# A tuned attention-and-MLP kernel: two token tiles of batch 1 as a quad of seven half-size products

## The chip, the cores and the metric

The kernel runs on one core of a Trainium2 chip. The metric is the device time of one execution in microseconds (us); several runs are made and their median is compared. Differences under about half a microsecond are close to what such runs can tell.

## The reference, cut to what matters

Four batches, eight heads, 768 tokens, head size 64, so a model width of 512. A block-sparse attention feeds an MLP over tokens and then over channels:

```python
scores = scale * q @ k^T                      # (4, 8, 768, 768), masked by blocks of 32
attn   = softmax(where(mask, scores, -1e9));  x = attn @ v        # (4, 768, 512)
a1  = alpha1 * x + beta1
tok = einsum('ts,bsd->btd', w_tok, a1);       u = x + lam * tok
a2  = alpha2 * u + beta2
ch  = maximum(a2 @ w_ch1, 0) @ w_ch2          # 512 -> 2048 -> 512
out = u + lam * ch
```

The change is in the last product, `relu(...) @ w_ch2`, of batch 1. `lam` is folded into the weights of that product beforehand (line 783), so a tile's product is simply added to `x_sb`, which holds u.

## The kernel before, in words

**Pairs and score groups.** Two heads are worked on at a time: 16 pairs, four to a batch. From pair 5 on, a pair is three *score groups*, and each group has three units of scores. TensorE writes the first unit into two tiles of the pool `mm` (two matmuls of 512 columns, or four of 256), and the other two into tiles of the pool `sp`. ScalarE takes the exponential (line 619): two instructions of 128x512 for the `mm` pair, one of 128x1024 for each `sp` tile. VectorE multiplies each result `eT` by the mask (line 636), TensorE multiplies by v (line 671, 12 or 24 short matmuls into `op`), VectorE normalises into `x_sb` (lines 688, 689).

**Around them**, for the same or an earlier batch: the token product (line 846, 12 matmuls, called L846 here), its addition and cast (lines 858, 865), a transposing DMA `uraw<-ubf` on SyncE's queue (line 898), the scaling of what it brings (line 889, "uscale"), the first MLP product (line 919, four matmuls of 384 columns) with its ReLU on ScalarE (line 926), and the second MLP product (line 1058). The first MLP product of a batch has 32 pieces; a piece of it is called **f** here. The second, done directly, has for each of the six token tiles four pieces of four matmuls of 512 columns, called **g**; after the fourth VectorE adds the bank to `x_sb` (line 1067) and SyncE stores the tile (line 1071).

**Order.** There is no run-time choice: each engine takes its instructions in the order of emission. That order is written out by hand in `WEAVE`, one string of letters per score group. `W1` is for pairs 5 to 7, `W2` for pairs 8 to 11, `W2L` for pairs 12 to 15, `W3` for the rest. The letters that matter here: `q` scores of a group and the first exponential; `x` the next exponential; `k` a mask multiply; `p` a product with v; `f` and `g` the next piece of the first and second MLP product; `S` and `A` one VectorE sum for the quads (activations, weights); `Y` the copy of v; `T` a token product; `v` a uscale; `d` a transposing DMA; digits are planned odd jobs. Batch 1's MLP runs inside `W2` (its f pieces begin in the fifth string) and the beginning of `W2L`.

**Quads.** For batches 2 and 3 the kernel takes two token tiles together (before: tile t and t+3) and does the 2x2 block product in seven products in place of eight, each of eight matmuls of 256 columns (lines 1160 and 1170). It needs four sums of activations on VectorE (line 1144: two new tiles, X1 and X2, and two in place), four sums of the weights, T1 to T4 (line 1098, done once), and after each product an addition to `x_sb` (line 1180). Products 1, 6 and 5 build on one another in one bank, products 7 and 4 in another. Between two of them VectorE reads the bank, and the next must wait for that read.

**Banks.** The pool `mm` has three banks of PSUM, `sp` two tiles of two banks, `op` one. All of this shares `mm`: the first unit of every score group (two tiles), every f, every g, every token product. Which bank a tile gets is settled when the program is built; a tile waits until the last reader of its bank is done.

```python
    def mm_tile(shape=(P, DM), dt=FP):
        return psum.tile(list(shape), dt, name="mm", tag="mm", bufs=3)
```

Of the kernel before, what the change touches and what calls it, by code (L numbers as in the profile page):

```python
# [18 lines left out]
B = 4  # L19
H = 8  # L20
S = 768
# [4 lines left out]
DM = 512  # L26
P = 128
NT = S // P
# [38 lines left out]
]  # L67
W2L = [
# [18 lines left out]
]  # L87
STR = (2, 3)
HN = NH // 2
HC = DM // 2  # L90
FS = 6
# [157 lines left out]
def kernel(  # L249
# [16 lines left out]
    nc = tc.nc  # L266
# [194 lines left out]
    def sp_tile():  # L461
        return psum.tile([P, 2, 512], FP, name="sp", tag="sp", bufs=2)
# [6 lines left out]
    def mm_tile(shape=(P, DM), dt=FP):  # L469
        return psum.tile(list(shape), dt, name="mm", tag="mm", bufs=3)  # L470
# [103 lines left out]
    x_sbs = {}  # L574
# [540 lines left out]
    def a_of(b, t, name, r=slice(0, HN)):  # L1115
        if name in ("X1", "X2"):
            return xs[(b, t, name)][:, r]
        c, half = {"11": (0, 0), "12": (0, 1), "21": (1, 0), "22": (1, 1)}[name]
        return hts[(b, c)][:, HN * half + r.start : HN * half + r.stop, ts(t, P)]

    SOP = {
        1: ("X1", "21", "22", ALU.add),
# [5 lines left out]
    def job_s(b, t, n, r=slice(0, HN)):  # L1128
        dst, a, c, op = SOP[n]
        rows = range(r.start, r.stop)  # L1130
        for name in (a, c):
            if name[0] == "X":
                assert all(("S", b, t, int(name[1]), m) in did for m in rows)
            else:
                h, half = divmod(int(name) - 11, 10)
                assert all(("f", b, h, HN * half + m) in did for m in rows)
# [7 lines left out]
        nc.vector.tensor_tensor(  # L1144
            out=a_of(b, t, dst, r), in0=a_of(b, t, a, r), in1=a_of(b, t, c, r), op=op
        )
        did.update(("S", b, t, n, m) for m in rows)
# [8 lines left out]
        7: ("21", "T3", 3),  # L1156
    }
    banks = {}

    def mul(b, t, n, ps, start, cols=slice(0, HC)):  # L1160
        a, m, need = PROD[n]
        assert m in bq or all((m, r) in did for r in range(0, HN, 2))
        if need:
            assert all(("S", b, t, need, r) in did for r in range(HN))
        c, half = {"1": (0, 0), "X": (1, 0)}.get(a[0], (1, 0))
        if need == 0:
            h, half = divmod(int(a) - 11, 10)
            assert all(("f", b, h, HN * half + r) in did for r in range(HN))
        for r in range(HN):
            nc.tensor.matmul(  # L1170
                ps,
                a_of(b, t, a)[:, r],
                b_rows(m, r)[:, 0, cols],
                start=(start and r == 0),
                stop=(r == HN - 1),
                skip_group_check=True,
            )

    def plus(x, ps):
        nc.vector.tensor_tensor(out=x, in0=x, in1=ps, op=ALU.add)  # L1180

    def twice(ps):
        return ps.unsqueeze(1).broadcast_to([P, 2, HC])
# [1 line left out]
    lo, hi = slice(0, HC), slice(HC, DM)  # L1185

    def job_p(b, t, n):
        x = x_sbs[b]
        last = (b, t) == (B - 1, NT // 2 - 1)
        bk = banks.setdefault((b, t), {})  # L1190
        if n in (1, 2, 7):
            bk[n] = sp_tile()[:, 0] if n == 1 else mm_tile()[:]
        if n == 3 and not last and 2 not in bk:
            bk[2] = mm_tile()[:]
        if n == 1:
            mul(b, t, 1, bk[1][:, lo], True)
            plus(x[:, t, lo], bk[1][:, lo])
        elif n == 2:
            mul(b, t, 2, bk[2][:, lo], True)
            if last or b < B - 1:  # L1200
                plus(x[:, t, lo], bk.pop(2)[:, lo])
            if last:
                emit_store(b, t, lo)
        elif n == 6:
            mul(b, t, 6, bk[1][:, lo], False)
            plus(x[:, t + 3, lo], bk[1][:, lo])
        elif n == 7:
            mul(b, t, 7, bk[7][:, lo], True)
            plus(x[:, t + 3, hi], bk[7][:, lo])
        elif n == 5:  # L1210
            mul(b, t, 5, bk[1][:, lo], False)
            plus(x[:, t : t + 4 : 3, hi], twice(bk[1][:, lo]))
        elif n == 4:
            mul(b, t, 4, bk[7][:, lo], False)
            plus(x[:, t + 3, lo], bk[7][:, lo])
            emit_store(b, t + 3, slice(0, DM))
        elif last:
            for h in range(2):
                sl = slice(HC + h * P, HC + h * P + P)
                ps = (mm_tile(), op_tile([P, DM]))[h]  # L1220
                mul(b, t, 3, ps[:, sl], True, ts(h, P))
                plus(x[:, t, sl], ps[:, sl])
                emit_store(b, t, sl, (nc.sync, nc.scalar)[h])
        else:
            sl = hi if b < B - 1 else slice(0, DM)
            mul(b, t, 3, bk[2][:, hi], b < B - 1)
            plus(x[:, t, sl], bk[2][:, sl])
            emit_store(b, t, slice(0, DM))
        did.add((b, t, n))

    NPAIR = B * NP
# [34 lines left out]
    def start_mlp(b):  # L1266
# [16 lines left out]
        ]  # L1283
        todo["S"] += [lambda t=t, n=n, r=r: job_s(b, t, n, r) for t, n, r in S_ORDER[b]]

    REST = (6, 7, 5, 4, 3)
    P_ORDER = {
        2: [(0, g, "g") for g in range(4)]
        + [(t, 2) for t in (1, 2)]
        + [(3, g, "g") for g in range(4)]  # L1290
        + [(t, 1) for t in (1, 2)]
        + [(t, n) for t in (1, 2) for n in REST],
        3: [(t, n) for t in range(2) for n in (1, 2)]
        + [(t, n) for t in range(2) for n in REST]
        + [(2, n) for n in (1, 2) + REST],
    }
    ALL, R1, R2 = slice(0, HN), slice(0, HN // 2), slice(HN // 2, HN)
    S_ORDER = {
        2: [(t, n, ALL) for t in (1, 2) for n in (1, 2, 3, 4)],
        3: [(t, n, R1) for n in (1, 2, 3) for t in range(3)]  # L1300
        + [(t, n, r) for t in range(3) for n, r in ((1, R2), (2, R2), (3, R2), (4, ALL))],
    }

    def start_pair(i):
# [227 lines left out]
```

## Time and profile before

| | |
|---|---|
| median of 3 runs | 298.61 us (298.6 to 298.87) |
| the profiled execution | 298.76 us |
| its span in the profile | 297.1 us, so 1.66 us lie around the span |
| granted TensorE clock | 1.0 throughout |
| TensorE busy | 289.7 us, 98% of the span |
| VectorE, ScalarE, GpSimd busy | 237.8, 217.1, 109.8 us |

A row of a timeline gives the start, the busy time, the engine, the line and operation, the tiles, and how many instructions were merged; in brackets stands the idle time of the engine before it and what ended that. Ends of matmuls are modelled, so the busy time of a row reaches a little into the next row; the spacing of the starts is what a piece costs.

The score groups of the stretch in question are numbered here by their start on TensorE in the profile before: G1 at 134.56 us, G2 142.44, G3 148.73 (these are pair 10), G4 154.89, G5 159.38, G6 164.88 (pair 11, the end of `W2`), G7 170.21, G8 173.69, G9 184.40 (pair 12, the beginning of `W2L`), G10 188.21, G11 191.54, G12 196.74.

### The profile page before, as it was taken

To read this page: it belongs to the slowest core of one execution; us is meant where nothing else is said; L and a number is where in the kernel's file an instruction comes from. 1 tells how busy PE (TensorE), PEld (TensorE's weight loads), DVE (VectorE), ACT (ScalarE), POOL (GpSimd) and SP (SyncE) were. 2 spreads that over 40 slices of the span, in tenths; PEclk is the share of its full clock that TensorE was granted. 3 is DMA by queue.
4 is the path that set the end of the run, shared out by engine and by line. 5 is a ranking of instruction groups with operands and counts; after the bars stand their busy time and mean duration, and the time that the engine had idled before them with its cause. 6 is when DMAs were issued, how large, how long until landed. Compare 5 with 4: busy or idle time off the path is not lost.

```text
span 297.1 us, 7554 instructions
## 1 busy us (share of the span) xinstructions
PE 289.7 (98%) x3082; PEld 193.5 (65%) x3101; DVE 237.8 (80%) x485; ACT 217.1 (73%) x324; POOL 109.8 (37%) x149
## 2 busy tenths in 40 slices
PE   8999999999999999999999999999999999999995
PEld 3688888665567565565576466556576679665884
DVE  4988899995678796977878777895956899799774
ACT  4999999998899963999779581999869744576000
POOL 8997978632443710355323340335320300000000
PEclk9999999999999999999999999999999999999999
DMA  6999999992392995729955767745520211400032
GB/s 182 184 199 186 192 171 187 171 123 44 95 147 55 112 203 84 118 65 119 125 96 73 124 110 146 103 92 69 70 62 17 38 38 29 141 1 3 0 141 73
DMA packets 57274, 31.09 MB, mean 105 GB/s; under 512 B 37204, under 2 KB 54016, under 8 KB 57240
## 3 DMA queue, kind: packets, MB, share of 16 engines
q0 software_dynamic: 16752, 14.22, 34.4%
q1 hardware_dynamic: 40020, 15.92, 29.3%
q8 instruction: 24, 0.39, 0.6%
q10 hardware_dynamic: 468, 0.47, 0.5%
q14 instruction: 10, 0.08, 0.1%
HBM read 29.75 MB, written 6.29 MB: 121 GB/s over the span
## 4 chain that ended last, share of the span: by engine, by line
PE 84%; DVE 6%; DMA 4%; ACT 3%; issue 1%; POOL 1%; SPq 0%; POOLq 0%
PE mm L919 18%; PE mm L1058 13%; PE sp L601 10%; PE mm L846 8%; PE op L671 7%; PE mm L1170 5%; PE sp L1170 4%; PE mm L601 3%; DVE eT L636 3%; PE mm L822 3%; PE op L648 2%; DMA vr<-in_v_dram 2%; ACT eT L619 2%; PE mm L1016 2%; PE sp L1016 2%; DMA uraw<-ubf 2%
## 5 line engine op out<-in xcount | busy, mean ns | idle before, releaser
L619 ACT ACTIVATE eT<-sp,expb 128x1024 f16<-128x1024 f32 x111 | 118.4, 1120 | 2.1 <-PE sp L601 1.4
L636 DVE TENSOR_TENSOR eT<-eT,mask 128x1024 f16<-128x1024 f16 x99 | 80.6, 843 | 13.5 <-ACT eT L619 13.3
L919 PE MATMUL mm<-uT,w1b 128*128 128x384 bf16 x416 | 76.8, 326 | 0.4 <-ACT hts L926 0.3
L705 POOL TENSOR_TENSOR a1pp<-x_sb,vbc 128x384 bf16<-128x384 f32 x25 | 28.5, 1138 | 119.0 <-DVE x_sb L689 84.7
L619 ACT ACTIVATE eT<-mm,expb 128x512 f16<-128x512 f32 x66 | 41.7, 685 | 26.5 <-PE mm L601 26.3
L926 ACT ACTIVATE hts<-mm 128x384 bf16<-128x384 f32 x104 | 49.1, 502 | 13.3 <-PE mm L919 12.4
L919 PEld LDWEIGHTS <-w1b 128*128 128x128 bf16 x416 | 38.7, 98 | 26.4 <-issue 2.9
L1058 PE MATMUL mm<-w2b,hts 128*128 128x512 bf16 x205 | 52.2, 379 | 0.9 <-issue 0.2
L671 PEld LDWEIGHTS <-eT 128*128 128x128 f16 x792 | 29.8, 98 | 8.8 <-issue 1.7
L1058 PEld LDWEIGHTS <-hts 128*128 128x128 bf16 x224 | 19.8, 98 | 22.3 <-issue 3.9
L671 PE MATMUL op<-vext,eT 128*128 128x65 f16 x792 | 32.1, 194 | 0.4 <-DVE x_sb L689 0.3
L601 PE MATMUL sp<-qTs,kTs 88*128 88x512 bf16 (+1 forms) x120 | 26.9, 325 | 1.2 <-ACT eT L619 0.7
L706 POOL TENSOR_TENSOR a1pp<-a1pp,vbc 128x384 bf16<-128x384 bf16 x25 | 26.7, 1069 | 2.0
L846 PE MATMUL mm<-a1pp,wtokT 128*128 128x256 bf16 x216 | 25.9, 273 | 0.1
L846 PEld LDWEIGHTS <-wtokT 128*128 128x128 bf16 x216 | 20.6, 98 | 5.6 <-issue 1.8
L1170 PEld LDWEIGHTS <-hts 128*128 128x128 bf16 x208 | 19.5, 98 | 3.0 <-issue 0.3
L858 DVE TENSOR_TENSOR x_sb<-x_sb,mm 128x512 f32<-128x512 f32 x18 | 12.3, 686 | 9.9 <-PE mm L846 9.8
L601 PE MATMUL sp<-qhT,khT 64*128 64x256 bf16 (+1 forms) x176 | 19.8, 322 | 0.0
L601 PEld LDWEIGHTS <-khT 64*128 64x128 bf16 x264 | 10.6, 94 | 12.7 <-issue 9.2
L648 PEld LDWEIGHTS <-eT 128*128 128x128 f16 x360 | 14.9, 97 | 3.8 <-issue 0.3
L689 DVE TENSOR_TENSOR x_sb<-op,rcp 128x384 f32<-128x384 f32 x28 | 15.6, 558 | 1.0
L1067 DVE TENSOR_TENSOR x_sb<-x_sb,mm 128x512 f32<-128x512 f32 x14 | 9.6, 686 | 8.2 <-PE mm L1058 6.7
(135 smaller groups left out, 376.9 us busy)
## 6 DMA issues: line engine op xcount, KB each, us to landing
out_dram<-x_sb SPq DMA_DIRECT2D x23, 256.0 KB
qpad<-in_q_dram POOLq DMA_DIRECT2D x15, 192.0 KB, 4.6
kr<-in_k_dram POOLq DMA_DIRECT2D x15, 192.0 KB, 5.3
vr<-in_v_dram POOLq DMA_DIRECT2D x15, 192.0 KB, 6.3
w1b<-in_moe_w_ch_dram POOLq DMA_DIRECT2D x4, 512.0 KB, 9.2
w2b<-in_moe_w_ch_dram POOLq DMA_DIRECT2D x4, 512.0 KB, 7.7
hts<-in_moe_w_tok_dram POOLq DMA_DIRECT2D x2, 576.0 KB, 8.7
x_sb<-in_k_dram ACTq DMA_DIRECT2D x2, 192.0 KB
```

The lines of the kernel that those rows point to most:

```text
L601: nc.tensor.matmul(sp[jj][:, dst], lhsT, rhs, start=True, stop=True, skip_group_check=True,)
L619: nc.scalar.activation(dst, at, AF.Exp, bias=expb[:], scale=SCALE)
L636: nc.vector.tensor_mul(out=e, in0=e, in1=keep)
L648: nc.tensor.matmul(op[0][:, o, :], ets[u][:, jj, h * QB + n * P : h * QB + n * P + P], vexts[i % NVB][:, w, 2 * jp + jj, :], start=op[1] == 0,
L671: nc.tensor.matmul(op[0][:, o, :], ets[u][:, jj, h * QB + n * P : h * QB + n * P + P], vexts[i % NVB][:, w, 2 * jp + jj, :], start=op[1] == 0,
L705: eng.tensor_tensor(out=dst, in0=x_sbs[b][:, :, cols], in1=bc[0], op=ALU.mult)
L706: eng.tensor_tensor(out=dst, in0=dst, in1=bc[1], op=ALU.add)
L846: nc.tensor.matmul(ps[:, o], wtokT[:, os_, ts(2 * n + o, P)], a1pps[i][:, os_, :], start=(os_ == 0 and o == 0), stop=(os_ == NT - 1 and o ...
L919: nc.tensor.matmul(ps[:, 0:QC], w1b[:, dk, ts(n, P)], uTs[b][:, dk, ts(c, QC)], start=(dk == 0), stop=(dk == 3),)
L926: nc.scalar.activation(h_row(b, c, n), ps[:, 0:QC], AF.Relu)
L1058: nc.tensor.matmul(ps[:], ht[:, nk, ts(o % 3, P)], w2b[:, nk, :], start=(nk == 0), stop=(nk == NH - 1),)
L1170: nc.tensor.matmul(ps, a_of(b, t, a)[:, r], b_rows(m, r)[:, 0, cols], start=(start and r == 0), stop=(r == HN - 1), skip_group_check=True,)
```

## The change

Batch 1's tiles 0 and 1 become a quad; tiles 2 to 5 stay direct. The quads are now named by their two tiles, `(0, 1)`, `(1, 4)` and so on, where before `t` stood for `(t, t + 3)`; the quads of batches 2 and 3 do the same work as before. The new quad's products 1, 6 and 5 use a bank of the pool `mm`, where the older quads use one of `sp`. The strings of `W2` from the seventh on, and two of `W2L`, are rewritten:

- G1: two f come sooner in place of two g; one S.
- G2: two f in place of two g; one S at the end.
- G3: a g (now product 2) at its end.
- G4: the three A move away, two S and two g (products 1 and 6) come in.
- G5: three g (product 5 and two pieces of tile 2) and no f, before three g and two f.
- G6: three A come in; four g (the last two pieces of tile 2, products 7 and 3) and no f, before four g and one f.
- G7: two g (product 4, the first piece of tile 3) and no f, before one g and one f.
- G11: no g, before one.

```diff
 W2 = [
 ...
-    "q f L f 0 f k A A A A A A A A 1 f Y x f p g x f p f g k k 2",
-    "q x k x k Q 0 g 1 s f f g p 2 p f f k p",
-    "q T 0 k f 1 x k f T x f 2 p k K p",
-    "q A A A x 0 x T k 1 k f 2 k f Q f d p L",
-    "q x 0 x K k g d k s f g f 1 k p p g 2",
-    "q Y g x x k g k f 0 1 k 2 p g v g v",
+    "q f L f 0 f k A A A A A A A A 1 f f S Y x f p f x f p f k k 2",
+    "q x f k x f k Q 0 1 s f f p 2 p f f k S p",
+    "q T 0 k f 1 x k f T x f 2 p k K p g",
+    "q S S g x 0 x T k g 1 k f 2 k f Q f d p L",
+    "q x 0 x K k g d k s g 1 k p p g 2",
+    "q Y A A A g x x k g k 0 1 k 2 p g v g v",
 W2L = [
-    "q 0 p p g k x L x p f k 1 K 2 k",
+    "q 0 p p g k x L x p g k 1 K 2 k",
 ...
-    "q 0 p 1 g x k f K k x f p p k 2 f",
+    "q 0 p 1 x k f K k x f p p k 2 f",
 ...
-STR = (2, 3)
+STR = (1, 2, 3)
 ...
+    LATE = [(2, (1, 4)), (2, (2, 5))] + [(3, (o, o + 3)) for o in range(3)]
 ...
-        if n in (1, 2, 7):
-            bk[n] = sp_tile()[:, 0] if n == 1 else mm_tile()[:]
-        if n == 3 and not last and 2 not in bk:
-            bk[2] = mm_tile()[:]
+        if n == 1 and (b, t) in LATE:
+            bk[1] = sp_tile()[:, 0]
+        elif n in (1, 2, 7) or (n == 3 and not tail):
+            bk[n] = mm_tile()[:]
 ...
     P_ORDER = {
+        1: quad((0, 1), (2, 1, 6, 5))
+        + direct(2)
+        + quad((0, 1), (7, 3, 4))
+        + direct(3, 4, 5),
 ...
     S_ORDER = {
+        1: [((0, 1), n, ALL) for n in (1, 2, 3, 4)],
```

More of the change, by code (lines that the diff above doesn't have):

```diff
@@ L1117, in a_of, with a_ready @@
             return xs[(b, t, name)][:, r]
-        c, half = {"11": (0, 0), "12": (0, 1), "21": (1, 0), "22": (1, 1)}[name]
-        return hts[(b, c)][:, HN * half + r.start : HN * half + r.stop, ts(t, P)]
+        o, half = t[int(name[0]) - 1], int(name[1]) - 1
+        return hts[(b, o // 3)][:, HN * half + r.start : HN * half + r.stop, ts(o % 3, P)]
+    def a_ready(b, t, name, rows):
+        if name[0] == "X":
+            return all(("S", b, t, int(name[1]), m) in did for m in rows)
+        o, half = t[int(name[0]) - 1], int(name[1]) - 1
+        return all(("f", b, o // 3, HN * half + m) in did for m in rows)
     SOP = {
@@ L1130, in job_s @@
         rows = range(r.start, r.stop)
[L1131 to L1136, printed above, removed]
+        assert a_ready(b, t, a, rows) and a_ready(b, t, c, rows)
         if n == 3:
@@ L1164, in mul @@
             assert all(("S", b, t, need, r) in did for r in range(HN))
[L1165 to L1168, printed above, removed]
+        assert a_ready(b, t, a, range(HN))
         for r in range(HN):
@@ L1221, in job_p @@
                 mul(b, t, 3, ps[:, sl], True, ts(h, P))
[L1222 to L1228 removed]
+                plus(x[:, o1, sl], ps[:, sl])
+                emit_store(b, o1, sl, (nc.sync, nc.scalar)[h])
+        else:
+            assert {(b, t, m) for m in (1, 2, 5)} <= did
+            sl, ps = (slice(0, DM), bk[2]) if tail else (hi, bk[3])
+            mul(b, t, 3, ps[:, hi], not tail)
+            plus(x[:, o1, sl], ps[:, sl])
+            emit_store(b, o1, slice(0, DM))
         did.add((b, t, n))
```

56 lines of the change are left out of this document (34 added, 22 removed).

## The prediction

> **What bounds the kernel now.** The first part of the page, the busy times, comes first: TensorE has no room.
>
> ```profile
> span 297.1 us, 7554 instructions
> PE 289.7 (98%) x3082; PEld 193.5 (65%) x3101; DVE 237.8 (80%) x485; ACT 217.1 (73%) x324; POOL 109.8 (37%) x149
> ```
>
> A busy share can hide waits, so the chain of waits gives the price of each piece, and the timeline of TensorE the starts of the score groups.
>
> ```profile
> 112.88 1.31 PE mm L846 x12
> 125.15 1.30 PE mm L919 x8
> 154.23 0.73 PE op L671 x24
> 182.74 1.73 PE mm L1058 x8
> 248.18 0.87 PE sp L1170 x8
> ```
>
> ```profile
> 135.32 3.42 PE L919 MATMUL mm<-uT,w1b 128*128 128x384 bf16 x20
> 142.44 0.39 PE L601 MATMUL mm<-qhT,khT 64*128 64x512 bf16 x2
> 142.66 0.60 PE L601 MATMUL sp<-qhT,khT 64*128 64x256 bf16 x6
> 148.73 0.39 PE L601 MATMUL mm<-qhT,khT 64*128 64x256 bf16 x4
> 170.21 0.39 PE L601 MATMUL mm<-qhT,khT 64*128 64x512 bf16 x2
> 173.69 0.39 PE L601 MATMUL mm<-qhT,khT 64*128 64x512 bf16 x2
> 184.40 0.39 PE L601 MATMUL mm<-qhT,khT 64*128 64x256 bf16 x4
> 195.25 0.91 PE L671 MATMUL op<-vext,eT 128*128 128x65 f16 x24 [0.25 <-DVE x_sb L689]
> 196.74 0.39 PE L601 MATMUL mm<-qhT,khT 64*128 64x256 bf16 x4
> ```
>
> An f costs 0.65 us, a g 0.865, a half-size product 0.87, twelve products with v 0.37, the scores of a group 0.22 + 0.60 = 0.82. G2 to G3 holds two g, four f and 36 products with v: 1.73 + 2.60 + 1.10 + 0.82 = 6.25 against 6.29 measured. So between 135 and 184 nothing is lost, and removed TensorE work is worth its length, if nothing else comes late. One place does lose: G9 to G12 takes 12.34, and its pieces (six g, three f, 72 products with v, three score groups: 5.19 + 1.95 + 2.19 + 2.46 = 11.8) leave about 0.5 of waiting, half of it the 0.25 shown.
>
> **What the change removes.** Eight g become seven products: 8 x 0.865 - 7 x 0.87 = **-0.83 us** on TensorE (eight half-size matmuls of 0.109). The Trainium skill, *TensorE: Matmul & The Clock Gate*, section *Back-to-back issue gap*, speaks against it: sustained spacing is about 131 ns at 512 columns and 81 at 128, which, interpolated, is an estimate of 98 at 256, so that the quad would cost 1.3 us more, not less. The rows above (216 and 109 ns) halve exactly and decide.
>
> **What it adds to VectorE, and what covers it.**
>
> ```profile
> L1144 DVE TENSOR_TENSOR xs<-hts 128x1024 bf16<-128x1024 bf16 x2 | 1.4, 682 | 0.0
> L1180 DVE TENSOR_TENSOR x_sb<-x_sb,mm 128x256 f32<-128x256 f32 x15 | 6.2, 417 | 1.4 <-PE mm L1170 1.4
> L1067 DVE TENSOR_TENSOR x_sb<-x_sb,mm 128x512 f32<-128x512 f32 x14 | 9.6, 686 | 8.2 <-PE mm L1058 6.7 <-PE sp L601 0.9 <-PE mm L919 0.5
> ```
>
> Four sums at 0.68, six additions at 0.42 and one at 0.69 come, two at 0.69 go: **+4.6 us**. In the windows it has room, and so has ScalarE after 140 us, but not before:
>
> ```profile
> core 0: us, PE busy (x) PEld busy (x) DVE busy (x) ACT busy (x) POOL busy (x), PEclk, DMA share, GB/s
> 135.00:140.00 5.00, 4.95 (x43) 2.85 (x39) 4.55 (x13) 4.55 (x10) 2.91 (x5) 1.00 1.17 147
> 140.00:145.00 5.00, 5.00 (x42) 2.62 (x41) 3.73 (x6) 4.02 (x7) 2.53 (x2) 1.00 1.39 126
> 145.00:150.00 5.00, 4.95 (x64) 3.29 (x63) 3.27 (x6) 3.73 (x8) 0.31 (x2) 1.00 0.79 147
> 165.00:170.00 5.00, 4.84 (x39) 2.43 (x36) 3.25 (x7) 3.66 (x5) 0.43 (x1) 1.00 0.93 167
> ```
>
> ```profile
> 141.24 0.37 DVE L329 COPY vext<-vr 128x768 f16<-128x768 f16 x1 [1.51 <-DMA vr<-in_v_dram]
> ```
>
> The first sum stands just before this copy and fits into its 1.51 of waiting; the second precedes the last 12 products with v of G2. I cost both at nothing; uncovered, 0.6 each. Product 6 must wait until VectorE has read product 1. Behind it on VectorE stand the token addition and the masks, ahead of it the addition of product 2 and two sums (0.42 + 1.36); twelve L846 matmuls, 1.31 us, lie between, so that even 0.42 for the read leaves some 0.8. Product 5 has three f between, product 4 a whole score group. The three moved A feed product 7, with a mask, an addition and two g between. All at nothing; if VectorE is late by 1 us, each of these waits costs up to 0.5. GpSimd's order does not move. On SyncE's queue three stores now stand together, the last waiting for product 4, ahead of the three transposing loads for G10, of which this is the last now:
>
> ```profile
> 177.60 2.28 SPq L570 DMA_TRANSPOSE qhT<-qpad x1
> 188.19 4.60 DMA uraw<-ubf
> ```
>
> With a landing like that of the other transposing DMA below it, it is there at 184.5, 3.7 before G10; about 1.5 later costs nothing.
>
> **Where TensorE will wait: three shortages of banks and one queue.** I followed the built order of the changed kernel, with the bank that each `mm` tile got, against these rows.
>
> ```profile
> 138.13 0.49 ACT L926 ACTIVATE hts<-mm 128x384 bf16<-128x384 f32 x1 [0.16 <-PE mm L919]
> 138.52 1.11 ACT L619 ACTIVATE eT<-sp,expb 128x1024 f16<-128x1024 f32 x1
> 139.51 0.49 ACT L926 ACTIVATE hts<-mm 128x384 bf16<-128x384 f32 x1
> 139.88 1.13 ACT L619 ACTIVATE eT<-sp,expb 128x1024 f16<-128x1024 f32 x1
> 142.86 1.27 ACT L619 ACTIVATE eT<-mm,expb 128x512 f16<-128x512 f32 x2 [0.69 <-PE mm L601]
> 144.02 2.12 ACT L619 ACTIVATE eT<-sp,expb 128x1024 f16<-128x1024 f32 x2
> 158.47 1.27 ACT L926 ACTIVATE hts<-mm 128x384 bf16<-128x384 f32 x3
> L619 ACT ACTIVATE eT<-mm,expb 128x512 f16<-128x512 f32 x66 | 41.7, 685 | 26.5 <-PE mm L601 26.3
> ```
>
> ScalarE's own spacing: 0.39 for a ReLU, 1.0 for an `sp` exponential, 0.58 for one of an `mm` pair; a ReLU starts 0.16 after its f.
>
> *(a) G1 to G3.* Four f replace four g; their ReLUs come while ScalarE is at its fullest. The fifth f ends at 138.58, as now. Then f to 139.23, v, f to 140.25, f to 140.90, v, f to 141.92, where G2 would start. ScalarE: fifth ReLU 138.76, exponential 139.15, two ReLUs from 140.15, exponential 140.92, next ReLU 141.92 to 142.41. G2's second tile lies in that ReLU's bank: 0.45 of waiting. In G2 the fourth f needs the bank of the first, whose ReLU stands behind an exponential and ends at 145.34, where TensorE would be at 145.15: with the hand-over 0.25. Sum **0.70**; bounds 0 (ScalarE half a microsecond earlier) and 0.9.
>
> *(b) G4 and G5.* The sums of products 1, 6 and 5 hold one bank of three. G4's three f go through two, and G5's second tile gets the bank of the last f, which has only twelve products with v (0.37) to be cleared in, against 0.16 + 0.49 and the hand-over: **0.30**; bounds 0 and 0.5.
>
> *(c) G7.* Product 7's bank is held until product 4, product 3's is not yet free, so both tiles of G7's first unit got the same third bank. The second score matmul waits until ScalarE has read the first, and all of TensorE behind it. No group of the kernel before is built so. From scores to exponential is 142.86 - 142.44 = 0.42, the exponential 0.685, while the two matmuls now run beside each other: 0.42 + 0.685 + about 0.05 for the hand-over - 0.11 (half of the pair's 0.22) = **1.05**. ScalarE is free by then: from G6's start it needs 0.42 + 1.16 + 2.1 = 3.7, TensorE 0.82 + 1.73 + 0.37 + 1.74 = 4.66. The exponential alone, 0.70, is the floor; 1.25 the ceiling. This one is structural. The Trainium skill, *Perfetto Trace Analysis*, section *Optimizing Tensor Performance*, states it as a rule: independent groups should rotate through banks, so that clearing one overlaps the next. By it the wait is one whole clearing; no row of the kernel before shows such a pair.
>
> *(d) G11 to G12.*
>
> ```profile
> 187.09 0.69 DVE L1067 TENSOR_TENSOR x_sb<-x_sb,mm 128x512 f32<-128x512 f32 x1 [0.28 <-PE mm L1058]
> 192.81 0.48 DVE L889 TENSOR_SCALAR uT<-uraw,ab2T 128x768 bf16<-128x768 bf16 x1 [0.62 <-DMA uraw<-ubf]
> 193.21 1.28 DVE L636 TENSOR_TENSOR eT<-eT,mask 128x1024 f16<-128x1024 f16 x2
> 194.63 0.56 DVE L689 TENSOR_TENSOR x_sb<-op,rcp 128x384 f32<-128x384 f32 x1
> ```
>
> G11 loses its g, the last tile's end moves ahead, and its addition now stands between the two mask multiplies and `x_sb`; batch 2's second f waits for that addition (same bank). Counted from G9's start: tile 4's addition was at 2.7 and comes one g sooner, so the transposing DMA behind its store goes out at 2.8 rather than 3.8. It lands at 7.4; uscale to 7.85, two masks to 9.05, the addition to 9.65, reciprocal and `x_sb` to 10.4. TensorE has three score groups, five g, 48 products with v and one f before that second f: 2.46 + 4.33 + 1.46 + 0.65 = 8.9. So it waits 0.8 there and hardly after, with the hand-over 0.9 in place of 0.5: **+0.4**; bounds -0.5 (the old wait goes too) and 0.7.
>
> **Sum.** -0.83 + 0.70 + 0.30 + 1.05 + 0.40 = +1.62 us. The profiled execution would go from 298.76 to 300.4; the median shown lies 0.15 below it, so I say **300.2**. With all terms at their lower or at their upper bound it is 298.0 or 301.1; the main case by itself 299.3 to 301.0.
>
> **Rivals.**
>
> 1. *ScalarE keeps up* (no difference): (a), (b) and (d) cost nothing, only (c) stands. For it: ScalarE has 0.98 of 5 free in 140 to 145, and matmul ends are modelled. Against it: the exponentials in front of the ReLUs. -0.83 + 1.05 = +0.2: 298.8. Chance 0.17.
> 2. *Hand-overs are shorter than the modelled ends say* (faster): each exponential and ReLU begins and frees its bank about 0.45 earlier relative to its matmul. Then (a) and (b) vanish, (c) falls to its floor 0.70, and the old wait before G12 goes as well: -0.83 + 0.70 - 0.5 = -0.63, so 298.0. It decides where a bank is free before the modelled end of what fills it plus the reader's row; the 0.42 from scores to exponential speaks against that. Chance 0.06.
> 3. *VectorE falls behind* in G4 to G7: products 6, 5, 4 and the direct tile behind them each wait 0.4 more, +1.6 on the main case: 301.8. Its 1.75 of 5 free in 165 to 170 speaks against it. Chance 0.05.
> 4. *Half-size products do not halve* among other work, say because a weight load cannot hide: at 0.124 per matmul the quad saves nothing (32 x 0.216 / 56), and the time is 301.0. The Trainium skill's spacings above point this way, the row at 248.18 does not. Chance 0.02.
>
> The main case has 0.70. A measurement can tell 0.2%, 0.6 us, from no change. So faster 0.06 (rival 2), within 0.2% 0.17 (rival 1), slower 0.77 (the rest). The range that holds eight in ten reaches from rival 1's lower half to the upper end of the main case and just past it: 298.7 to 301.2.
>
> **What would show it.** Right: in G7, one `mm` score matmul, an exponential of 128x512, then the second, with an ACT wait near 1 us on TensorE; L1058 down by 32 matmuls, and seven more rows of eight half-size ones; G3 about 0.2 earlier than 148.73, where work alone would make it 0.8; G8 near 175.7 (as many g and f stand before it as now, so 173.69 would move by (a), (b) and (c) alone); the second f of batch 2 waiting for L1067. Wrong: G7 closed up in 0.82, G3 at 147.9, or the span below 297.

## The result and the profile after

The changed kernel takes **300.75 us** (median of 6 runs, 300.5 to 301.66) against 298.83 for the kernel before (6 runs on the same chip, 298.6 to 299.14): a ratio of 1.0071, with a 95% interval of 1.0061 to 1.0082 (the ratios here are estimated from the single runs, so they are not quite those of the medians). It is 1.9 us slower; the forecast was 300.2, within 298.7 to 301.2. The profiled execution took 300.69 with a span of 299.0, 1.9 over the span before.

The page's first part, after:

```profile
span 299.0 us, 7614 instructions
PE 290.9 (97%) x3110; PEld 196.2 (66%) x3125; DVE 240.9 (81%) x494; ACT 217.6 (73%) x324; POOL 109.9 (37%) x149
```

TensorE is busy for 1.2 us longer although 0.83 of work has gone from it: the record of a matmul reaches beyond the start of the next (a score matmul is 0.39 long, and the piece behind a pair starts after 0.22), so a short wait disappears in it, and matmuls that no longer run two at a time, as after a torn pair below, count as busy. The busy share does not show these waits. The view of waits names only two, and one engine for each:

```profile
PE mm L601 <- ACT eT L619: 0.8, 1, 0.8
PE mm L919 <- DVE x_sb L1067: 0.7, 1, 0.7
```

The timeline of TensorE shows all of them, to be read by the starts of the score groups (start, length of the row, then the instruction and in brackets the idle time ahead of it):

```profile
134.63 0.39 PE L601 MATMUL mm<-qhT,khT 64*128 64x512 bf16 x2
...
142.07 0.84 PE L601 MATMUL mm<-qhT,khT 64*128 64x512 bf16 x2
142.54 0.80 PE L601 MATMUL sp<-qhT,khT 64*128 64x256 bf16 x6
143.28 3.00 PE L919 MATMUL mm<-uT,w1b 128*128 128x384 bf16 x16
146.11 0.90 PE L671 MATMUL op<-vext,eT 128*128 128x65 f16 x24
...
148.61 0.39 PE L601 MATMUL mm<-qhT,khT 64*128 64x256 bf16 x4
...
156.40 1.05 PE L1169 MATMUL mm<-w2b,hts 128*128 128x256 bf16 x8
157.29 1.47 PE L846 MATMUL mm<-a1pp,wtokT 128*128 128x256 bf16 x12
...
159.47 2.20 PE L919 MATMUL mm<-uT,w1b 128*128 128x384 bf16 x12
...
161.97 0.65 PE L601 MATMUL mm<-qhT,khT 64*128 64x512 bf16 x2
...
171.13 0.39 PE L601 MATMUL mm<-qhT,khT 64*128 64x512 bf16 x1
172.30 0.37 PE L601 MATMUL mm<-qhT,khT 64*128 64x512 bf16 x1 [0.78 <-ACT eT L619]
...
175.98 0.39 PE L601 MATMUL mm<-qhT,khT 64*128 64x512 bf16 x2
...
196.50 0.81 PE L919 MATMUL mm<-uT,w1b 128*128 128x384 bf16 x4 [0.69 <-DVE x_sb L1067]
...
198.70 0.39 PE L601 MATMUL mm<-qhT,khT 64*128 64x256 bf16 x4
```

Two marks of a wait that no bracket shows: a pair longer than the 0.39 of a free one (0.84 at 142.07, 0.65 at 161.97), and pieces longer than their price (the four f of 143.28 take 2.83 until the next operation at 146.11, where they are 2.60). At 171.13 G7 is torn in two, with 1.17 between its score matmuls. That is the sight that the prediction named, and so are the rest: G3 stands 0.12 earlier than before (0.2 was said), G8 at 175.98 (175.7), and at 196.50 batch 2's second f waits for L1067.

The readers of the banks, ScalarE for (a), (b) and (c), then VectorE for (d):

```profile
141.97 0.90 ACT L926 ACTIVATE hts<-mm 128x384 bf16<-128x384 f32 x2
161.71 0.49 ACT L926 ACTIVATE hts<-mm 128x384 bf16<-128x384 f32 x1 [0.25 <-PE mm L919]
171.56 0.69 ACT L619 ACTIVATE eT<-mm,expb 128x512 f16<-128x512 f32 x1 [1.42 <-PE mm L601]
172.71 0.69 ACT L619 ACTIVATE eT<-mm,expb 128x512 f16<-128x512 f32 x1 [0.46 <-PE mm L601]
```

```profile
195.78 0.67 DVE L1067 TENSOR_TENSOR x_sb<-x_sb,mm 128x512 f32<-128x512 f32 x1
```

In G7 ScalarE had been idle for 1.42 before the first exponential, and 0.05 after the end of that exponential (172.25) the second score matmul starts.

From group to group, start to start, in us (worked out from the rows of the score groups; "work" is what the edits move by the prices of the prediction, f 0.65, g 0.865, half-size product 0.87):

| | G1-2 | 2-3 | 3-4 | 4-5 | 5-6 | 6-7 | 7-8 | 8-9 | 9-12 | sum |
|---|---|---|---|---|---|---|---|---|---|---|
| before | 7.88 | 6.29 | 6.16 | 4.49 | 5.50 | 5.33 | 3.48 | 10.71 | 12.34 | 62.18 |
| after | 7.44 | 6.54 | 7.04 | 6.32 | 4.46 | 4.70 | 4.85 | 10.71 | 12.01 | 64.07 |
| difference | -0.44 | +0.25 | +0.88 | +1.83 | -1.04 | -0.63 | +1.37 | 0 | -0.33 | +1.89 |
| of it work | -0.43 | -0.43 | +0.87 | +1.74 | -1.30 | -0.64 | +0.22 | 0 | -0.865 | -0.83 |
| of it waiting | 0 | **0.68** | 0 | **0.09** | **0.26** | 0 | **1.15** | 0 | **0.54** | 2.72 |

From G12 to the end the two profiles agree to 0.05, so these 1.89 are the whole of it. The four waits stand where the prediction put (a), (b), (c) and (d). Below, a kernel is read by its length from G1 to G12 in its trace, since most stretches in which two kernels have the same order come out equal to 0.01 or 0.02 (G3 to G4 is 7.04 or 7.05 in ten of these kernels), where a timed ratio has an interval of some 0.3 us to each side. Stretches where an engine waits for a DMA do not: with the strings of the kernel before, G9 to G12 takes 12.34 there and 12.12 or 11.92 in runs below.

### The profile page after: what moved, and what is told of

Same layout as the page of the kernel before. It is cut to its first block, busy times and chain, and to the rows that moved or that the text cites. A ratio compares the mean times of both kernels' runs of the same rounds, so it can differ in the third digit from the quotient of the medians.

```text
span 299.0 us, 7614 instructions
## 1 busy us (share of the span) xinstructions
PE 290.9 (97%) x3110; PEld 196.2 (66%) x3125; DVE 240.9 (81%) x494; ACT 217.6 (73%) x324; POOL 109.9 (37%) x149
## 3 DMA queue, kind: packets, MB, share of 16 engines
HBM read 29.75 MB, written 6.29 MB: 121 GB/s over the span
## 4 chain that ended last, share of the span: by engine, by line
PE 84%; ACT 7%; DVE 6%; DMA 1%; issue 1%; ACTq 0%
PE mm L919 20%; PE mm L1058 12%; PE sp L601 10%; PE mm L846 8%; PE op L671 7%; PE mm L1169 7%; ACT eT L619 5%; PE sp L1169 4%; PE mm L601 3%; DVE eT L636 3%; PE mm L822 3%; PE mm L1016 2%; PE op L648 2%; PE sp L1016 2%; PE mm L648 1%; ACT hts L926 1%
## 5 line engine op out<-in xcount | busy, mean ns | idle before, releaser
L636 DVE TENSOR_TENSOR eT<-eT,mask 128x1024 f16<-128x1024 f16 x99 | 79.7, 830 | 13.7 <-ACT eT L619 13.5
L1058 PE MATMUL mm<-w2b,hts 128*128 128x512 bf16 x177 | 44.8, 379 | 0.7
L1058 PEld LDWEIGHTS <-hts 128*128 128x128 bf16 x192 | 17.0, 98 | 19.2 <-issue 3.3
L1169 PEld LDWEIGHTS <-hts 128*128 128x128 bf16 x248 | 23.2, 98 | 3.7 <-issue 0.6
L858 DVE TENSOR_TENSOR x_sb<-x_sb,mm 128x512 f32<-128x512 f32 x18 | 12.3, 685 | 10.8 <-PE mm L846 10.8
L601 PE MATMUL sp<-qhT,khT 64*128 64x256 bf16 (+1 forms) x176 | 20.4, 323 | 0.0
L601 PE MATMUL mm<-qhT,khT 64*128 64x512 bf16 (+1 forms) x88 | 14.0, 329 | 0.9 <-ACT eT L619 0.8
```

What stands on the lines that cost most here:

```text
L601: nc.tensor.matmul(sp[jj][:, dst], lhsT, rhs, start=True, stop=True, skip_group_check=True,)
L636: nc.vector.tensor_mul(out=e, in0=e, in1=keep)
L1058: nc.tensor.matmul(ps[:], ht[:, nk, ts(o % 3, P)], w2b[:, nk, :], start=(nk == 0), stop=(nk == NH - 1),)
L1169: nc.tensor.matmul(ps, a_of(b, t, a)[:, r], b_rows(m, r)[:, 0, cols], start=(start and r == 0), stop=(r == HN - 1), skip_group_check=True,)
```

## The experiments

Each run was timed beside the kernel before on its chip, whose medians there were 298.36 to 298.61.

**The shared bank, (c).** Two kernels. The first exchanges two products, so that G7's second score tile gets another bank than its first, though one that is read late:

```
-        + quad((0, 1), (7, 3, 4))
+        + quad((0, 1), (3, 7, 4))
```

> The changed kernel (300.75 us) with products 3 and 7 of the quad exchanged: 3 before the last products with v of G6, 7 behind them, so that of the two banks held at G7 one is product 3's, filled a product earlier. In the changed kernel G7's second score matmul starts at 172.30, 1.17 after the first, behind an exponential in the same bank. Theory (c) in its simple form, that the shared bank is all of it: G7's scores close up, 1.05 less, 299.7. The same theory with VectorE's order in it: product 3's addition stands on VectorE behind two mask multiplies, the reciprocal and x_sb, which ended at 171.6, so that its bank comes free at 172.05: the second score matmul starts at about 172.1, 0.2 less, 300.55. Rival (ScalarE is late by itself, whichever bank): no change, 300.75.

300.21 us, 1.0063 of before (1.0051 to 1.0075). TensorE, then VectorE:

```profile
170.87 0.39 PE L601 MATMUL mm<-qhT,khT 64*128 64x512 bf16 x1
171.83 0.37 PE L601 MATMUL mm<-qhT,khT 64*128 64x512 bf16 x1 [0.57 <-DVE x_sb L1179]
```

```profile
169.47 1.28 DVE L636 TENSOR_TENSOR eT<-eT,mask 128x1024 f16<-128x1024 f16 x2
...
171.37 0.41 DVE L1179 TENSOR_TENSOR x_sb<-x_sb,mm 128x256 f32<-128x256 f32 x1
```

The second score matmul starts 0.96 after the first in place of 1.17: 0.2 gained, the second of the two numbers, not the first. It now waits for product 3's addition, which VectorE makes from 171.37 to 171.78, behind the two masks of 169.47, the reciprocal and `x_sb`. A bank is free when its reader comes to it in its own queue, not when the product ends.

The second kernel also moves those two masks behind the additions:

```
-    "q Y A A A g x x k g k 0 1 k 2 p g v g v",
+    "q Y A A A g x x k g 0 1 2 p g g k k v v",
```

> As the run before this one, and besides the two last mask multiplies of G6 moved on VectorE behind the additions of products 3 and 7 (the scaling of batch 2's inputs stays behind them). Now product 3's addition can end at about 171.0, before G7 starts at 171.13. Theory (c): both score matmuls of G7 run side by side, 1.05 less than the changed kernel, 299.7 (299.4 to 300.0). Rival (ScalarE or VectorE is late by itself): the wait turns up again in G7 at the products with v, which need those masks, or in G8's scores, and less than 0.4 is gained: above 300.35.

299.62 us, 1.0044 (1.0032 to 1.0056).

```profile
170.93 0.39 PE L601 MATMUL mm<-qhT,khT 64*128 64x512 bf16 x2
...
174.78 0.39 PE L601 MATMUL mm<-qhT,khT 64*128 64x512 bf16 x2
```

G7's pair runs side by side, and G7 to G8 takes 3.85 in place of 4.85. Theory (c) holds at 1.00 of its 1.15; the remaining 0.15 lies at the two stretches of products with v, which need the masks that come later now.

**ScalarE's backlog, (a).** First the last two ReLUs of G1 go to VectorE:

```
+        if (b, c, n) in ((1, 1, 2), (1, 1, 3)):
+            nc.vector.tensor_scalar_max(out=h_row(b, c, n), in0=ps[:, 0:QC], scalar1=0.0)
+        else: nc.scalar.activation(...)
```

> The changed kernel with the ReLUs of two pieces of the first product (the last two of G1) on VectorE in place of ScalarE. Theory (a): ScalarE's backlog from G1 to G3 is 0.9 shorter, G2's second score matmul no longer waits, nor does the fourth piece in G2: 0.7 less, 300.05 (G3 at about 147.9 in place of 148.61). Rival (the wait is VectorE's or the queue's, not ScalarE's): G3 stays at 148.6 and the time at 300.75, or above, since VectorE's masks for G2's products with v come up to 0.9 later.

300.43 us, 1.0078 (1.0061 to 1.0096): no gain that the timing can tell. In the trace G2's pair is closed up again, but G2 to G3 takes 6.28, not 5.86: 0.26 gained, not 0.7. The fourth f still waits, for a ReLU behind G2's own exponentials:

```profile
143.63 1.11 ACT L619 ACTIVATE eT<-sp,expb 128x1024 f16<-128x1024 f32 x1
144.63 0.50 ACT L931 ACTIVATE hts<-mm 128x384 bf16<-128x384 f32 x1
```

So (a) is two waits, one from a backlog and one from an order. The next run also sets the order right, with the first f of G2 issued ahead of its second exponential:

```
-    "q x f k x f k Q 0 1 s f f p 2 p f f k S p",
+    "q f x k x f k Q 0 1 s f f p 2 p f f k S p",
```

> The changed kernel with the last two ReLUs of G1 on VectorE, as in the run with that alone (G3 moved from 148.61 to 148.33 there, not to 147.9: the fourth piece of G2 still waited 0.32 for the ReLU of the first, which stood behind an exponential of G2's own), and besides G2's first piece issued ahead of G2's second exponential, so that its ReLU stands before that on ScalarE. Theory (a) in its two parts, a backlog and an order: both waits go, G3 comes at 147.9, 0.7 less than the changed kernel: 1.2 above the kernel before. Rival (what is short is ScalarE's time in G2, not the order): the wait moves to the products with v of G2, whose exponential comes 0.4 later, and G3 stays at 148.3: 1.6 or more above the kernel before.

300.55 us, 1.0070 (1.0056 to 1.0084); G2 to G3 6.13. Of the 0.68, 0.41 is gone. Of the 0.27 that is left, 0.1 comes with the cure itself: G2's first f starts at 143.07, behind a ReLU that VectorE makes from 142.46 to 143.01. The other 0.17 is the rival's: the fifth and sixth f of G2 now stretch (1.47 for 1.30), since the exponential that was passed comes later:

```profile
146.40 1.63 PE L919 MATMUL mm<-uT,w1b 128*128 128x384 bf16 x8
147.87 0.53 PE L671 MATMUL op<-vext,eT 128*128 128x65 f16 x12
```

Around the start of G2 ScalarE has no time to spare. The windows of the changed kernel say so, with ScalarE busy for the whole of 140 to 145, where before it had 0.98 free:

```profile
core 0: us, PE busy (x) PEld busy (x) DVE busy (x) ACT busy (x) POOL busy (x), PEclk, DMA share, GB/s
140.00:145.00 5.00, 4.92 (x42) 2.79 (x41) 4.10 (x7) 5.00 (x10) 2.52 (x2) 1.00 1.37 143
```

**The last addition, (d).** First the last piece of tile 5 goes back from G10 into G11:

```
-    "q 0 p k x v Q v 1 2 p k x g k g",
-    "q 0 p 1 x k f K k x f p p k 2 f",
+    "q 0 p k x v Q v 1 2 p k x g k",
+    "q 0 p 1 g x k f K k x f p p k 2 f",
```

> The changed kernel with the last piece of direct tile 5 moved back from the end of G10 into G11, where the kernel before has it. Nothing is added or taken away. Theory (d): its addition stands behind the masks and x_sb on VectorE again, the second piece of batch 2's first product waits 0.5 in place of 0.85 with the piece of 0.865 as cover: 0.4 less, 300.35 (0.3 to 0.5). Rival (the wait is the masks' own, set by the transposing DMA, and comes whatever stands in front): 300.75.

300.45 us, 1.0079 (1.0062 to 1.0097); G9 to G12 11.92 in place of 12.01. The 0.4 did not come. The wait before the second f is gone, but another stands in its place:

```profile
194.53 0.39 PE L601 MATMUL mm<-qhT,khT 64*128 64x512 bf16 x2
194.81 0.40 PE L601 MATMUL sp<-qhT,khT 64*128 64x256 bf16 x4
195.82 0.39 PE L601 MATMUL sp<-qhT,khT 64*128 64x512 bf16 x2 [0.61 <-ACT eT L619]
```

G10, shorter by a piece, no longer covers ScalarE's exponentials, and G11's scores wait 0.6 for one of them. This run does not decide on (d); it shows what else that piece was good for. The next takes the spare place out of G8, which is long, and leaves G10 alone:

```
-    "q Q 0 g x g f v v s T T x k 1 k p p g g T g g Y d 2 k",
+    "q Q 0 g x g f v v s T T x k 1 k p p g g T g Y d 2 k",
-    "q 0 p 1 x k f K k x f p p k 2 f",
+    "q 0 p 1 g x k f K k x f p p k 2 f",
```

> The changed kernel with G11 given back its piece of direct tile 5, and the piece that is one too many taken out of G8 (10.7 us long) in place of G10, which in the run that took it there left G11's scores waiting 0.61 for ScalarE. Theory (d): tile 5's addition stands behind the masks and x_sb again, G9 to G12 takes 12.3 as in the kernel before and G8 0.865 less, 0.5 less than the changed kernel in all: 1.4 above the kernel before. Rival (that wait hangs on the transposing DMA and not on the addition): what G8 gives, G11 takes, and the time stays 1.9 above the kernel before.

299.76 us, 1.0039 (1.0027 to 1.0051), better than expected. G8 to G9 is 0.86 shorter, and G9 to G12 takes 11.92 with a piece of 0.865 more than the changed kernel has in it: 0.95 of waiting is gone, the 0.54 of the change and the 0.42 that the kernel before has there too. The rival's form, what G8 gives G11 takes, did not come; but two things changed at once, the addition's place and the landing of the transposing DMA, which VectorE did not wait for here.

**All four at once.** The three cures above with those for (b):

```
-    "q S S g x 0 x T k g 1 k f 2 k f Q f d p L",
-    "q x 0 x K k g d k s g 1 k p p g 2",
+    "q S S g x 0 x f T k f 1 k g 2 k Q d p L",
+    "q x 0 x K k g f d k s g 1 k p p g 2",
```

> The changed kernel with all four waits taken away: two ReLUs of G1 on VectorE and G2's first piece ahead of its second exponential (a); in G4 and G5 a piece of the first product between product 1 and the token matmuls, one between them and product 6, the third behind product 5 in G5, so that no piece stands right before G5's scores (b); products 3 and 7 exchanged and G6's last two masks behind their additions (c); the spare place in G8 and not in G11 (d). Theory: 2.7 of waits go from 1.9 above the kernel before: 0.8 below it, 298.0 against 298.83. If the terms are not independent (a wait that goes uncovers another) it lies between: each 0.3 uncovered costs as much. Rival (the earlier pieces and the sums lengthen the kernel by themselves): at or above the kernel before.

298.45 us, 0.9999 of before (0.9991 to 1.0008): what the change lost is won back, and no more. G1 to G12 is 61.89, 0.29 below before. G4 had got a new wait, of the second f for the first one's ReLU, which stood behind the exponentials:

```profile
157.45 1.47 PE L846 MATMUL mm<-a1pp,wtokT 128*128 128x256 bf16 x12
159.29 0.81 PE L919 MATMUL mm<-uT,w1b 128*128 128x384 bf16 x4 [0.37 <-ACT hts L931]
```

So G4 was laid out once more, with one piece behind the token matmuls and two in G5:

```
+    "q S S g x 0 x T k f 1 k g 2 k Q d p L",
+    "q x 0 x K k g d k s f g f 1 k p p g 2",
```

> The run with all four waits taken away came level with the kernel before, not 0.8 below: its trace shows G4 and G5 losing 0.52 where the early piece's ReLU stood behind G4's exponentials, so that the next piece waited for its bank. Here G4 has one piece, between the token matmuls and product 6, and the other two stand in G5 as in the kernel before; all else as in that run. Theory (waits on held banks, each set by where a ReLU or an addition stands in its queue): that 0.52 goes and nothing takes its place, 0.5 below the kernel before (0.3 to 0.7). Rival (ScalarE or VectorE as a whole sets the time in G4 to G6, so that a wait taken away there comes back a group later): level with the kernel before.

298.34 us, 0.9997 (0.9988 to 1.0006); G1 to G12 61.92. G4 to G6 takes 10.79 where the run before it took 10.96. G4's wait is gone and G5's pair is free, but product 5 waits 0.2 for VectorE's addition and the last f of G5 0.1: of the 0.52, 0.17 was gained, and the rest came back nearby, as the rival says. The changed kernel takes 10.78 in G4 to G6, so the cures for (b) took its waits away and won no time there. G2's first f also waits 0.2 for its ReLU on VectorE, which this edit does not touch: VectorE stood behind the load of v, whose copy starts at 140.81 in both runs, and all else in G1 came 0.22 earlier here. Without that the trace would lie 0.5 below the kernel before, as the theory said; the times cannot tell.

**Each part alone.** The earlier pieces without a quad: the kernel before with the f and A of G1 to G8 at the changed kernel's places, and direct pieces where the products stand.

> The other part of the change alone: the kernel before (tiles 0 and 1 direct, no quad, no S sums), with the pieces of the first product and the T sums at the changed kernel's places in G1 to G8 and the direct pieces in the places of the quad's products. TensorE's work is that of the kernel before. Theory: (a) and (b) belong to the order of the pieces and come without a quad, (c) and (d) do not come (no bank is shared in G7, and G11 keeps its piece): 0.7 + 0.3 = 1.0 above the kernel before (0.7 to 1.2). Rival (the quad's sums on VectorE are what makes ScalarE's and VectorE's readers late in G1 to G5): at most 0.3 above the kernel before.

300.15 us, 1.0052 (1.0040 to 1.0064): slower by 1.6, where the theory says 1.0 (1.17 in the trace from G1 to G12). G2 to G3 is 6.53 and the pairs of G2 and G5 are as long as in the changed kernel:

```profile
141.90 0.84 PE L601 MATMUL mm<-qhT,khT 64*128 64x512 bf16 x2
...
161.77 0.65 PE L601 MATMUL mm<-qhT,khT 64*128 64x512 bf16 x2
```

So (a) and (b) come from the order of the pieces, and neither products nor sums are needed for them. By the prices above they make 0.67 and 0.33, the 1.0 of the theory. G7 shows no torn pair; G8 has 0.39 of waiting of its own, and G9 to G12 is 0.22 shorter than before.

And the quad without anything sooner: direct tile 2 first, then the seven products in the places of G5 and G6. The strings are those of the kernel before, but for the four S in G3 to G5, the two last masks of G6 behind product 3's addition, and one g less in G8.

```
-        1: quad((0, 1), (2, 1, 6, 5)) + direct(2) + quad((0, 1), (7, 3, 4)) + direct(3, 4, 5),
+        1: direct(2) + quad((0, 1), (2, 1, 6, 5, 7, 3, 4)) + direct(3, 4, 5),
```

> The quad of tiles 0 and 1 with nothing sooner: direct tile 2 takes the places that direct tile 0 has in G1 and G2 of the kernel before, the pieces of the first product and of the T sums stay where that kernel has them, the four S sums stand in G3 to G5, the seven products in the seven places of G5 and G6, and of the piece places one in G8 falls away (G11 keeps its own). In G6 the two last masks stand behind product 3's addition on VectorE. No bank is held over G7 but one that its scores do not take. Theory (the loss is in the four waits (a) to (d), which hang on where pieces and held banks lie, and the work term is real): (a), (b), (c) and (d) are gone and the work of 0.83 comes off the kernel before: 0.83 below it, 298.0 against 298.83 (down to -0.4 if product 1's bank, held from G5 to G6, costs 0.4). Rival (a quad among these score groups loses its saving whatever its order, since it fills VectorE and banks): at or above the kernel before, 298.8 to 299.5.

299.06 us, 1.0018 (1.0008 to 1.0028), 1.6 below the changed kernel but not below the kernel before. (a) and (b) are gone to 0.03, and so is the torn pair of G7. New are two waits, 0.76 in G6 (6.11 to G7 where its work is 5.35) for VectorE's addition, and 0.63 in G8 (10.48 where its work is 9.85), 0.43 of it between the two score matmuls, for a ReLU:

```profile
165.07 0.39 PE L601 MATMUL mm<-qhT,khT 64*128 64x256 bf16 x4
...
166.57 1.03 PE L1169 MATMUL mm<-qTs,xs 128*128 128x256 bf16 x8 [0.69 <-DVE x_sb L1179]
...
174.65 0.39 PE L601 MATMUL mm<-qhT,khT 64*128 64x512 bf16 x1
175.30 0.37 PE L601 MATMUL mm<-qhT,khT 64*128 64x512 bf16 x1 [0.27 <-ACT hts L926]
```

VectorE's timeline has no gap from 154 to 166, with three A and all four sums in that stretch: this is the prediction's rival 3, in another order than the one it was priced for. With the A in G3, the sums in G1, G2, G4 and G6, and the f of G7 exchanged for a piece of G8 (three of the strings):

```
+    "q T A A A 0 k f 1 x k f T x f 2 p k K p",
+    "q S x 0 x T k 1 k f 2 k f Q f d p L",
+    "q Y g S x x k g f 0 1 2 p g k k v g v",
```

> The quad with nothing sooner came 0.5 above the kernel before, not 0.8 below: its trace shows product 5 waiting 0.75 in G6 for the addition of product 6, which stood on VectorE behind three T sums and all four S sums between G3 and G6 (VectorE without a gap from 153 to 166), and 0.43 in G8 for the ReLU of the piece right before it. Here the three T sums stand in G3, where VectorE has 1.46 of waiting, the S sums in G1, G2, G4 and G6, and the piece of G7 in G8 (a direct piece takes its place). Theory (work that comes off TensorE counts in full where VectorE's queue does not stand before a held bank): 1.2 less than that run, 0.7 below the kernel before (0.4 to 1.2, with the 0.4 that G9 to G12 gave in that run). Rival (the 3 to 4 us of additions and sums on VectorE cannot be hidden in G1 to G8): at or above the kernel before.

297.97 us (median of 12, 297.81 to 299.52) against 298.57, a ratio of 0.9988 (0.9974 to 1.0002). G1 to G12 takes 61.55, 0.63 less than before, about what the medians differ by; the interval just reaches no change. It is the best of these kernels, and it is not shown to be faster. Of these 0.63, 0.42 is the old wait in G9 to G12 (11.92 for 12.34). Of the 0.83 of work some 0.2 is left, and the rest is lost again to small waits, the largest 0.15 in G3 and 0.36 in G5. A last run put the A ahead of G3's token addition and product 2's addition ahead of a mask:

```
-    "q T A A A 0 k f 1 x k f T x f 2 p k K p",
+    "q A A A T 0 k f 1 x k f T x f 2 p k K p",
-    "q x 0 x K k g d k s f g f 1 k p p g 2",
+    "q x 0 x K g k d k s f g f 1 k p p g 2",
```

> The second run of the quad with nothing sooner came some 0.5 below the kernel before (298.0 against 298.6). What is left in its trace: 0.14 at G3's last products with v and 0.34 in G5, where the second piece waits for product 2's bank, whose addition stood on VectorE behind a mask multiply that took 1.42 beside GpSimd's work in place of 0.68. Here the three T sums stand ahead of G3's token addition on VectorE, in its 1.45 of waiting, and product 2's addition ahead of that mask. Theory (only where an addition or a sum stands in VectorE's queue matters): another 0.5 less, 1.0 below the kernel before (0.6 to 1.2). Rival (VectorE has no time left in G3 to G6, so that the masks come later by as much): 0.5 below, as that run.

298.59 us, 1.0002 (0.9993 to 1.0011): 0.5 lost in place of 0.5 won. VectorE, GpSimd and TensorE in G3:

```profile
149.44 1.56 DVE L1098 TENSOR_TENSOR qk<-w2b 128x512 bf16<-128x512 bf16 x2
150.92 1.14 DVE L1098 TENSOR_TENSOR tmore<-w2b 128x512 bf16<-128x512 bf16 x1
151.98 0.68 DVE L858 TENSOR_TENSOR x_sb<-x_sb,mm 128x512 f32<-128x512 f32 x1
```

```profile
149.67 1.05 POOL L705 TENSOR_TENSOR a1pp<-x_sb,vbc 128x384 bf16<-128x384 f32 x1 [4.76 <-DVE x_sb L689]
150.79 0.98 POOL L706 TENSOR_TENSOR a1pp<-a1pp,vbc 128x384 bf16<-128x384 bf16 x1
```

```profile
152.71 1.47 PE L846 MATMUL mm<-a1pp,wtokT 128*128 128x256 bf16 x12 [0.53 <-DVE x_sb L858]
```

The three A took 2.6 where they take 1.1 elsewhere, because GpSimd's two multiplications lie at the same time (in the run before they stood behind those, at 153.14, and took 1.1), and the second token group waited 0.53 for the addition behind them. VectorE's 1.45 of waiting in G3 was not free time.

## Why the prediction was right

**The sum.** It said -0.83 of work and 2.45 of waiting; the trace has -0.83 and 2.72. Each term, as put there, against the table:

- *Work, -0.83.* The prices hold to 0.02: between other pieces a half-size product takes 0.87 to 0.89 from start to start (156.40 to 157.29 is the longest), a g 0.865, and eight g are gone. No run shows the 0.83 as time won. Rival 4 is out, and with it the spacing of the Trainium skill that the prediction quoted from *TensorE: Matmul & The Clock Gate*, section *Back-to-back issue gap*: here 0.109 to 0.111 per half-size matmul stands in place of an estimated 0.098, and 0.216 in place of 0.131 at full size.
- *(a) G1 to G3, 0.70.* Measured 0.68, where it was put (0.45 expected and 0.46 measured from G2's start to its first f, 1.21 where the scores of G1 take 0.75 until the next piece, start to start; the prediction's 0.82 for them goes by the length of a row; 0.25 and 0.23 for the fourth f). The ReLU that it placed at 141.92 to 142.41 is the first of the row of 141.97. Its cause is shown for 0.41 by the two ReLU runs, 0.26 as a backlog and 0.15 as an order; of the remaining 0.27, 0.17 lies behind an exponential on ScalarE and 0.1 came with the cure, so for this part the cause is argued. It is caused by the earlier pieces alone, as the run without a quad shows.
- *(b) G4 and G5, 0.30.* Measured 0.35: 0.26 at G5's pair, where it was put, and 0.09 at G4's f, which had no price. It also comes without the quad, so "the sums of the products hold one bank" was too narrow: a direct tile in the same place holds one as well. Both waits go where no piece of the first product stands right before G5's scores, but in the kernels that keep the rest of the change others as long or longer come instead.
- *(c) G7, 1.05.* Measured 1.15. The second matmul starts 1.17 after the first, as put (0.42 + 0.685 + 0.05); the 0.1 more lies in the last term, which put 0.11 for the second score matmul. Behind a free pair the other six matmuls of the group start two at a time (176.21, 176.32 and 176.43 in G8) and take 0.53 until the next piece. In G7 the second one starts beside the first of them (172.30), the rest follow singly, and the next piece comes after 0.74. The same 0.2 is in G2 and G5 (142.54 to 143.28, 162.26 to 162.99): here a torn pair costs it beside its wait, and in (a) it makes up nearly half of the 0.46. (c) is the largest of the four, and does not come with the earlier pieces alone. It goes when the second tile gets a bank that is free in time, and by only 0.2 when it gets one that is read late. The rule that the prediction quoted from the Trainium skill, *Perfetto Trace Analysis*, section *Optimizing Tensor Performance*, gives no time; taken as one whole clearing it agrees, an exponential of 0.69 and what lies around it, 1.17 between the two matmuls.
- *(d) G11 to G12, +0.40.* Measured 0.54: a new wait of 0.95 in place of an old one of 0.42, where it said 0.9 in place of 0.5. The row of 196.50 names the addition, and in both runs with the addition back behind `x_sb` no f waits for it. The way there was in part luck: the prediction had VectorE wait for the transposing DMA, with the scaling done 7.85 after G9's start. It was done at 7.88, but VectorE came to it straight from its masks (no bracket at 193.79) and waited for no DMA. The old wait goes with that DMA: it was there 4.60 after its issue before, with VectorE idle for 0.62 and G9 to G12 at 12.34; at most 4.4, 0.40 and 12.12 in the run with the earlier pieces alone; at most 4.0, no idle time and 11.92 with the piece out of G8. Why the landing differs is open.

**VectorE at nothing.** Right for this order: product 6 starts at 158.60, right behind the token matmuls, and product 5 (162.99), 7 (169.29) and 4 (173.78) each right behind what stands before it on TensorE. The load was put too high: VectorE's busy time rose by 3.1 (237.8 to 240.9), not by 4.6. That it costs nothing was not right in general, as the quad with nothing sooner shows with 0.76. The margin was an order, and not the 1.75 of 5 free that the prediction quoted.

**The rivals.** Rival 1 (ScalarE keeps up) is refuted by the waits of (a) and (b) and by the window with no time left on ScalarE; rival 2 (shorter hand-overs) by 0.05 from the end of the exponential to the matmul behind it in G7 (172.25 to 172.30) and by (c) at 1.15; rival 3 did not come in the changed kernel.

**What was missed** is not in the prediction but in the first idea drawn from it, that four waits taken away give 0.83 below the kernel before. They won back the 1.9 that the change had lost, and below that 0.3 in the trace and nothing that the timing can tell. Even these 0.3 are less than the old wait of 0.42 in G9 to G12, which went as well. A cure moved pieces that had covered something else, so the terms of the sum cannot be taken out one by one.

## What to carry to other kernels

When TensorE's work is cut by less than 1 us in a kernel whose order is written out by hand, count the readers of its banks first: for each group, which bank the next tile gets, what stands ahead of its reader on ScalarE or VectorE, and what TensorE has to do in the meantime. A bank that is held across a group of scores can cost a whole exponential, more than the cut is worth. A piece moved earlier or later takes its cover and its reader's load with it, so look at the group that it leaves as well as at the one that it enters.

## What was not expected of the hardware

VectorE's operations with two inputs in SBUF took up to about twice their time while GpSimd multiplied. In the trace of the kernel before, 66 mask multiplies with no multiplication of GpSimd beside them took 0.68 to 0.69, and 30 that lay mostly beside one took up to 1.49, 1.18 in the mean. Two in the best of the kernels here took 1.42 and 1.08:

```profile
162.18 1.42 DVE L636 TENSOR_TENSOR eT<-eT,mask 128x1024 f16<-128x1024 f16 x1 [0.21 <-ACT eT L619]
163.51 0.41 DVE L1179 TENSOR_TENSOR x_sb<-x_sb,mm 128x256 f32<-128x256 f32 x1
163.84 1.08 DVE L636 TENSOR_TENSOR eT<-eT,mask 128x1024 f16<-128x1024 f16 x1
164.84 0.41 DVE L1179 TENSOR_TENSOR x_sb<-x_sb,mm 128x256 f32<-128x256 f32 x1
```

```profile
162.04 1.00 POOL L705 TENSOR_TENSOR a1pp<-x_sb,vbc 128x384 bf16<-128x384 f32 x1 [9.35 <-DVE x_sb L689]
163.12 1.25 POOL L706 TENSOR_TENSOR a1pp<-a1pp,vbc 128x384 bf16<-128x384 bf16 x1
```

The additions between them, whose second input lies in PSUM, keep their 0.41. The Trainium skill, *SBUF — State Buffer*, section *Who interferes with whom*, says that a VectorE instruction with two inputs in SBUF contends with a GpSimd instruction that reads SBUF, and that one with at most one such input does not, outside the two-port modes; these rows agree. The scaling of line 889, with one such input, took 1.05 in place of 0.47 in the changed kernel (171.96), beside a multiplication of GpSimd; no run shows in which mode it works. The contention is what made the three A of the last run so long, and it means that a gap of VectorE beside GpSimd's work is worth about half its length for such operations.

Some executions also came to G1 later than the rest by 0.9 to 1.6 us, with nothing in their order changed there (135.50 and 136.18 in two of the profiles, against 134.33 to 134.76 in the others). No run here tells why; it is another reason to compare from G1 on.
